# Top-32 search over halves of a score row: larger halves first, then larger and smaller together

## The chip, the core and the metric

The kernel runs on one core of a Trainium2 chip. The metric is the device time in microseconds (us) of one execution, as the median of several. PE is the matmul engine, PEld its weight loads, DVE the vector engine, ACT the scalar engine, POOL the GpSimd engine and SP the engine whose queue issues most DMAs.

## What is computed

```
# q, k, v: (B=8, H=8, S=576, D=64); TOPK = 32
scores = (1/8) * q @ k^T                         # 576 scores in a row
kth    = 32nd largest score of each row
attn   = softmax(scores where scores >= kth, else -1e9)
x      = (attn @ v) as (B*S = 4608, H*D = 512)
h      = x @ w_in                                # w_in: 512 x 2048
out    = (h * cos(h)) @ w_out                    # w_out: 2048 x 512
```

## The kernel before

**Units and slots.** The work of the attention is cut into 144 units: 128 rows of tokens by two heads. Four units, one for each pair of heads, make one block of 128 tokens, and there are 36 blocks. A loop by hand writes one slot for each unit. In slot i, `u` is unit i (its search), `w` is unit i-1 (its softmax), `x` is unit i-2 (its transposition) and `z` is a group of four units whose product with v is due, in every slot with i mod 4 = 2 from slot 10 on (slot 5 has the first group). There is no scheduler: each engine does its instructions in the order in which `slot` writes them, and waits for others by semaphores.

**A slot.** `scores` lets PE write a row's 576 scores of two heads to PSUM, the tile `sc` (columns 0 to 447) and the tile `rim` (the rest). Even slots write the scores of the next two units. `sc` has two buffers, so the second of the two waits until DVE has folded unit i. `take_scores` (L253, L257) copies the scores of unit i+1 to SBUF on ACT, the tile `s`; its copy from `rim` comes after the products with v, which also lie in `rim`. `mask` (L378) and `exponentials` (L387) are ACT's too. `split` (L410, L412) lets POOL part the finished weights into 16-bit halves; `write_halves` and `transposes` (L441, L447) send them by DMA to DRAM and back, transposed, into `ring`, on SP's queue. `values` (L475) multiplies them by v. `send` is split, write, due loads and transposition in one. Slots 0 to 5 use `turn`, a transposition on PE, in place of `send`.

**The search.** A row is folded: `fold_high` (L267, DVE) writes the larger of columns j and j+288, 288 numbers, to the second half of the tile `rest`. `fold_sum` and `fold_low` (L283, L292, POOL) make the smaller of each two from integer sums: a + b - max. In slots 8 to 10 (`BUSY`) `fold_now` (L275, DVE) makes it. Then DVE searches with MAX8 (L359, the eight largest of a row) and MATCH_REPLACE8 (L364, strikes these out; a MATCH_VALUE_LOAD goes ahead of each), each for two heads: four rounds over the 288 larger ones, which give 32, and two rounds over the 288 smaller ones, which give 16. At most 16 of the smaller can be among the 32 largest. `merge_first` and `merge_second` (L347, L352) find the 32nd largest from both sorted lists, in the next slot.

**The second part.** `ff1` (L554) and `ff2` (L630) are the products with w_in and w_out. ACT takes `ff1`'s results (L568, L570), POOL reduces them to a range (L590, L599), ACT takes the sine (L609), POOL multiplies (L616). `plan` says how many items of each kind PE gets in each slot.

**The weights.** w_in and w_out come as 64-bit numbers. In the first slots they are decoded: ACT in `decode_first` (L133, L136), DVE in `decode_second` (L151), POOL in `decode_third` (L160). In slots from 2 on, DVE's and POOL's parts are written after `topk_round(u, 2)`; in slot 0 at the slot's end and in slot 1 ahead of the last search. POOL's part of slots 0 to 9 has 3, 3, 4, 3, 4, 4, 3, 2, 2 and 2 instructions, and that of slot 11 two.

Of the kernel before, what the change touches and what calls it, by code (L numbers as in the profile page):

```python
# [10 lines left out]
F32 = mybir.dt.float32  # L11
I32 = mybir.dt.int32
# [3 lines left out]
ALU = mybir.AluOpType  # L16

P = 128
TOPK = 32
NEG = -3.4028234663852886e38  # L20
# [10 lines left out]
def kernel(  # L31
# [9 lines left out]
    nc = tc.nc  # L41
    ctx.enter_context(tc.manual_schedule())
    B, H, D, S = qT.shape
# [4 lines left out]
    NP = H // 2  # L48
    NF = DF // P
    HS = S // 2  # L50
# [33 lines left out]
    for i in range(DF // CW):  # L84
        w = consts.tile([P, NC, CW], F32, tag=f"w_in{i}", name=f"w_in{i}")
# [4 lines left out]
    w = consts.tile([P, NF, DM], F32, tag="w_out", name="w_out")  # L90
# [4 lines left out]
    BUSY = range(8, 11)  # L95
# [154 lines left out]
    def take_scores(u):  # L250
# [7 lines left out]
        if at:  # L258
            nc.scalar.copy(out=s[:, :, 0:at], in_=u["sc"][:, :, 0:at])  # L259

    def fold_high(u):

        s, sc = u["s"], u["sc"]
        if u["n"] not in BUSY:
            del u["sc"]
        u["rest"] = work.tile([P, 2, S], F32, tag="rest", name="rest", bufs=1)
        nc.vector.tensor_tensor(  # L267
            out=u["rest"][:, :, HS:S], in0=sc[:, :, 0:HS], in1=s[:, :, HS:S], op=ALU.max
        )

    def fold_now(u):

        s, sc = u["s"], u.pop("sc")
        u["low"] = work.tile([P, 2, HS], F32, tag="low", name="low", bufs=1)
        nc.vector.tensor_tensor(  # L275
            out=u["low"], in0=sc[:, :, 0:HS], in1=s[:, :, HS:S], op=ALU.min
        )

    def fold_sum(u):

        s = u["s"].bitcast(I32)
        u["low"] = work.tile([P, 2, HS], F32, tag="low", name="low", bufs=1)
        nc.gpsimd.tensor_tensor(  # L283
            out=u["low"].bitcast(I32), in0=s[:, :, 0:HS], in1=s[:, :, HS:S], op=ALU.add
        )

    def fold_low(u):

        if u["n"] in BUSY:
            return  # L290
        low = u["low"].bitcast(I32)
        nc.gpsimd.tensor_tensor(  # L292
            out=low, in0=low, in1=u["rest"][:, :, HS:S].bitcast(I32), op=ALU.subtract
        )

    dens = []
    for i in range(2):
        t = consts.tile([P, 2, 2], F32, tag=f"dens{i}", name=f"dens{i}")
# [2 lines left out]

    tops = []
    for i in range(2):
        t = consts.tile([P, 2, TOPK + 1, 2], F32, tag=f"top{i}", name=f"top{i}")
        nc.vector.memset(t[:, :, 0, 1], -NEG)
        tops.append(t)

    def topk_first(u, w):  # L310

        u["top"] = tops[u["n"] % len(tops)]
        if w:
            merge_first(w)
        if u["n"] not in BUSY:
            fold_sum(u)
        fold_high(u)
        if w:
            merge_second(w)
        if u["n"] in BUSY:  # L320
            fold_now(u)
        topk_round(u, 0, [lambda: distances(w), lambda: None] if w else ())

    def topk_round(u, rnd, between=(), ahead=None):
        top, rest, lasts = u["top"], u["rest"], TOPK // 8 - 1
        end = TOPK - 1 - 8 * rnd
        at = top[:, :, end : end - 8 if rnd < lasts else None : -1, 0]
        search(
            at, rest[:, :, HS:S] if rnd == 0 else rest[:, :, 0:HS], rest[:, :, 0:HS], rnd < lasts,
            between if rnd < lasts else (),  # L330
        )
        if rnd < lasts:
            return
        del u["rest"]
        low = u.pop("low")
        for k in range(TOPK // 16):
            more = k < TOPK // 16 - 1
            if ahead and not more:
                ahead()
            search(top[:, :, 1 + 8 * k : 9 + 8 * k, 1], low, low, more, () if more else between)  # L340

    def merge_first(u):
        n = TOPK // 2 + 1
        u["lesser"] = u["top"].rearrange("p j r i -> p j (r i)")[:, :, 2 * n : 3 * n]
        nc.vector.tensor_reduce(  # L347
            out=u["lesser"], in_=u["top"][:, :, 0:n], axis=mybir.AxisListType.X, op=ALU.min
        )

    def merge_second(u):
        nc.vector.tensor_reduce(  # L352
            out=u["top"][:, :, TOPK - 1, 1], in_=u.pop("lesser"), axis=mybir.AxisListType.X,
            op=ALU.max, negate=True,
        )

    def search(to, src, rest, more, between=()):
        for j in range(2):
            nc.vector.max(to[:, j], src[:, j])  # L359
            if between:  # L360
                between[j]()
        if more:
            for j in range(2):
                nc.vector.match_replace(rest[:, j], to[:, j], src[:, j], NEG)  # L364

    def distances(u):
        top = u.pop("top").rearrange("p j r i -> p j (r i)")
        u["less"] = top[:, :, 2 * TOPK - 1 : 2 * TOPK]
        u["nd"] = small.tile([P, 2], F32, tag="nd", name="nd")
        nc.vector.tensor_reduce(  # L370
            out=u["nd"], in_=top[:, :, 2 * TOPK - 2 : 2 * TOPK], axis=mybir.AxisListType.X, op=ALU.add
        )

    def mask(u):
# [46 lines left out]
    def turn(u):  # L421

        s = u.pop("s").rearrange("p j k -> p (j k)")
        pT = u["pT"] = ring[:, u["n"] % RING]
        for half in range(2):
            tt = ps.tile([P, 512], F32, tag="mm", name="tt", bufs=2)
            for c in range(NT):
                at = (half * NT + c) * P
                nc.tensor.transpose(tt[:, c * P : (c + 1) * P], s[:, at : at + P], ident)
            nc.scalar.copy(out=pT[:, half * NT : (half + 1) * NT], in_=tt.rearrange("p (c q) -> p c q", c=NT))  # L430
        at = 2 * NT * P
        nc.tensor.transpose(room[0][:, P : 2 * P], s[:, at : at + P], ident)
# [307 lines left out]
    def send(x):  # L740

        split(x)
        write_halves(x)
        for load, b, hp in at_send.pop(x["n"] + 2, ()):
            load(b, hp)
        transposes(x)
# [8 lines left out]
    def slot(i, u, w, x, z):  # L755
        n = (3, 4, 3, 4, 4, 3)[i] if i < NP + 2 else 2 if i != 2 * NP + 1 else 0
        if i < NP:
            for load, b, hp in at_once[i]:
                load(b, hp)
        load_weights(n, nc.sync if i < NP + 2 else nc.scalar)  # L760
        if x:
            (turn if i < NP + 2 else send)(x)
        ff["late"] = False
        topk_first(u, w)
        fold_low(u)
        topk_round(u, 1)
        topk_round(u, 2)
        if i > 1:
            decode_second(NP)
            decode_third()  # L770
        reduce_first()
        reduce_second()
        made = scored.get(i, [])
        if z:
            take_banks()
        feed(*((0, 0) if i == NP + 2 else plan[i % NP][0]))

        for m in made:
# [46 lines left out]
    def drain(w, x, z):  # L825

        take_banks()
        if x:
            send(x)
        if w:  # L830
            merge_first(w)
            merge_second(w)
            distances(w)
            mask(w)
            exponentials(w)
            sums(w)
            reciprocal(w)
        forward(2)
        if z:
            values(z)  # L840
            take_values(z)
        forward(2)
# [60 lines left out]
```

## Time and profile before

| | |
|---|---|
| median of 3 runs | 1400.27 us (1400.18 to 1404.11) |
| the profiled execution's own time | 1399.15 us |
| its span, first to last instruction | 1397.0 us |
| granted PE clock, mean over the span | 0.974 |
| PE busy | 1339.6 us, 96% |
| DVE busy | 1334.2 us, 96% |
| POOL busy | 1169.3 us, 84% |
| ACT busy | 1140.6 us, 82% |

Of the profiled execution's own time 2.15 us lie outside its span. A busy share is an average over the whole span; the stages differ, and the sums below are made by stage. Instructions of DVE overlap a little, so the mean duration of one is longer than the step from one start to the next.

### The profile page before, as it was taken

To read this page: it belongs to the slowest core of one execution; us is meant where nothing else is said; L and a number is where in the kernel's file an instruction comes from. 1 tells how busy PE (TensorE), PEld (TensorE's weight loads), DVE (VectorE), ACT (ScalarE), POOL (GpSimd) and SP (SyncE) were. 2 spreads that over 40 slices of the span, in tenths; PEclk is the share of its full clock that TensorE was granted. 3 is DMA by queue.
4 is the path that set the end of the run, shared out by engine and by line. 5 is a ranking of instruction groups with operands and counts; after the bars stand their busy time and mean duration, and the time that the engine had idled before them with its cause. 6 is when DMAs were issued, how large, how long until landed. Compare 5 with 4: busy or idle time off the path is not lost.

```text
span 1397.0 us, 43804 instructions
## 1 busy us (share of the span) xinstructions
PE 1339.6 (96%) x17024; PEld 905.7 (65%) x17024; DVE 1334.2 (96%) x5004; ACT 1140.6 (82%) x2043; POOL 1169.3 (84%) x804
## 2 busy tenths in 40 slices
PE   5558999999999999999999999999999999999998
PEld 3445666666666666666666666666666666666664
DVE  7999999999999999999999999999999999999931
ACT  7987888888888888888888888888888888888842
POOL 4778988889988888888988889888888898998820
PEclk6688999999999999999999999999999999999999
DMA  9566776777575586658756567676766566555530
GB/s 303 180 203 179 196 191 167 202 175 206 160 179 160 154 198 177 175 161 200 185 157 170 159 178 191 177 164 171 211 163 172 160 171 163 160 146 157 157 103 16
DMA packets 427487, 240.86 MB, mean 172 GB/s; under 512 B 375952, under 2 KB 392592, under 8 KB 427280
## 3 DMA queue, kind: packets, MB, share of 16 engines
q1 hardware_dynamic: 420720, 224.22, 61.0%
q10 hardware_dynamic: 6560, 13.85, 2.9%
q8 instruction: 133, 2.18, 0.7%
q14 instruction: 74, 0.61, 0.1%
HBM read 45.09 MB, written 101.19 MB: 105 GB/s over the span
## 4 chain that ended last, share of the span: by engine, by line
PE 59%; DVE 35%; ACT 2%; DMA 2%; POOL 1%; issue 1%; SPq 0%; DVEq 0%; POOLq 0%; ACTq 0%
PE o L630 23%; PE mm L554 23%; DVE top L359 16%; DVE rest L364 10%; PE rim L475 7%; PE sc L242 5%; DVE low L364 3%; DVE rest L267 3%; PE rim L242 1%; DMA ring<-rows 1%; DMA rows<-halves 1%; DVE xT L491 0%; DVE top L347 0%; DVE w_out L151 0%; DVE top L352 0%
## 5 line engine op out<-in xcount | busy, mean ns | idle before, releaser
L554 PEld LDWEIGHTS mm<-xT,w_in 128*64 128x64 f32 x9216 | 512.8, 137 | 85.1 <-issue 57.2
L554 PE MATMUL mm<-xT,w_in 128*64 128x128 f32 x9216 | 528.7, 273 | 3.2 <-DVE xT L491 2.1
L630 PE MATMUL o<-w_out,g 128*64 128x512 f32 x2304 | 520.0, 594 | 0.0
L359 DVE MAX8 top<-rest 128x8 f32<-128x288 f32 x1152 | 479.5, 452 | 0.0
L364 DVE MATCH_REPLACE8 rest<-top,rest 128x288 f32<-128x288 f32 x864 | 377.0, 444 | 0.0
L378 ACT ACTIVATE s<-s,top 128x576 f32<-128x576 f32 x288 | 207.7, 768 | 160.8 <-DVE top L352 157.8
L630 PEld LDWEIGHTS o<-w_out,g 128*64 128x64 f32 x2304 | 158.6, 137 | 254.1 <-issue 253.1
L410 POOL COPY halves<-s 128x2304 uint16<-128x2304 uint16 x140 | 294.8, 2106 | 29.1 <-ACT s L387 26.0
L359 DVE MAX8 top<-low 128x8 f32<-128x288 f32 x576 | 242.6, 452 | 0.4 <-POOL low L292 0.4
L387 ACT ACTIVATE s<-s,nd 128x576 f32<-128x576 f32 x288 | 220.5, 769 | 1.1
L292 POOL TENSOR_TENSOR low<-low,rest 128x576 int32<-128x576 int32 x141 | 199.6, 1416 | 11.1
L283 POOL TENSOR_TENSOR low<-s 128x576 int32<-128x576 int32 x141 | 199.7, 1417 | 6.1 <-ACT s L259 6.1
L599 POOL TENSOR_TENSOR x<-g,x 128x1024 f32<-128x1024 f32 x68 | 161.6, 2376 | 5.7
L242 PE MATMUL sc<-k,q 64*64 64x448 f32 (+1 forms) x1120 | 146.9, 568 | 16.9 <-DVE low L275 10.2
L616 POOL TENSOR_TENSOR g<-g,x 128x1024 f32<-128x1024 f32 x68 | 161.7, 2378 | 0.0
L475 PE MATMUL rim<-ring,v 128*64 128x128 f32 (+1 forms) x2560 | 138.3, 267 | 0.0
L475 PEld LDWEIGHTS rim<-ring,v 128*64 128x64 f32 x2560 | 129.2, 139 | 6.5 <-issue 6.0
L253 ACT COPY s<-sc 128x896 f32<-128x896 f32 (+1 forms) x144 | 128.4, 891 | 3.1 <-PE sc L242 3.1
L257 ACT COPY s<-rim 64x256 f32<-64x256 f32 (+1 forms) x280 | 102.9, 368 | 29.5 <-PE rim L475 27.9
L364 DVE MATCH_REPLACE8 low<-top,low 128x288 f32<-128x288 f32 x288 | 125.8, 446 | 0.0
L267 DVE TENSOR_TENSOR rest<-sc,s 128x576 f32<-128x576 f32 x144 | 107.7, 748 | 7.0 <-ACT s L259 6.4
L568 ACT ACTIVATE g<-mm 128x512 f32<-128x512 f32 x144 | 85.2, 592 | 25.7 <-PE mm L554 23.2
(55 smaller groups left out, 1161.8 us busy)
## 6 DMA issues: line engine op xcount, KB each, us to landing
rows<-halves SPq DMA_DIRECT2D x140, 640.0 KB, 3.5
out_dram<-ob ACTq DMA_DIRECT2D x36, 256.0 KB, 2.2
q<-in_q_dram SPq DMA_DIRECT2D x31, 288.0 KB, 4.6
st<-in_moe_w_in_dram SPq DMA_DIRECT2D x16, 512.0 KB, 5.1
v<-in_v_dram SPq DMA_DIRECT2D x32, 256.0 KB, 4.2
k<-in_k_dram SPq DMA_DIRECT2D x31, 144.0 KB, 4.2
k<-in_k_dram SPq DMA_DIRECT2D x32, 128.0 KB, 4.7
st<-in_moe_w_out_dram SPq DMA_DIRECT2D x8, 512.0 KB, 4.7
```

Source lines behind the costliest of these rows:

```text
L242: nc.tensor.matmul(to[r0 : r0 + rows, rim_bank(r0, j) if k0 else place(u["hp"], j), 0 : k1 - k0], st["q"][d, q0 : q0 + rows], st["k"][d, k ...
L283: nc.gpsimd.tensor_tensor(out=u["low"].bitcast(I32), in0=s[:, :, 0:HS], in1=s[:, :, HS:S], op=ALU.add)
L292: nc.gpsimd.tensor_tensor(out=low, in0=low, in1=u["rest"][:, :, HS:S].bitcast(I32), op=ALU.subtract)
L359: nc.vector.max(to[:, j], src[:, j])
L364: nc.vector.match_replace(rest[:, j], to[:, j], src[:, j], NEG)
L378: nc.scalar.activation(out=s[:, j], in_=s[:, j], func=AF.Prelu, bias=less[:, j], scale=1.0, alpha=FAR)
L387: nc.scalar.activation(out=s[:, j], in_=s[:, j], func=AF.Exp, bias=nd[:, j : j + 1], scale=SCALE, accum_out=den[:, j, 0:1],)
L410: nc.gpsimd.tensor_copy(out=halves[:, :, 0 : 2 * S], in_=s.rearrange("p (k h) -> p h k", h=2))
L475: nc.tensor.matmul(to[d, r], lhsT, rhs, start=(bank, j) not in begun, stop=c == NT - 1 and u in us[-2:] and r0 + rows == P,)
L554: nc.tensor.matmul(mm[r0 : r0 + D, at : at + w], w_in[f // FC][:, c, (f % FC) * P + r0 : (f % FC) * P + r0 + D], blk["xT"][:, c], start=c ...
L616: eng.tensor_tensor(out=g, in0=g, in1=x, op=ALU.mult)
L630: nc.tensor.matmul(o[r0 : r0 + D], g[:, at + r0 : at + r0 + D], w_out[f], start=f == 0, stop=f == NF - 1)
```

## The change

The four rounds become these: the first over the 288 larger numbers (now the tile `high`), whose remainder is written to the first half of `rest`; the second over that remainder, 288 wide; the third and fourth over both halves of `rest` together, 576 wide, larger and smaller. The smaller numbers are therefore read from the third round on, where they were read after the fourth. The last number found is the threshold, and `threshold` (one reduction) takes the place of the two merges.

The function `by_vector` makes DVE fold the smaller numbers also in slots 13, 17, 21 and so on (i mod 4 = 1), beside slots 8 to 10. From slot 6 on, where POOL folds, `send(x)` is now written after the folds; where DVE folds, it stays ahead of the search.

```diff
+    def by_vector(u):
+        return u["n"] in BUSY or (u["n"] > max(BUSY) and u["n"] % NP == 1)
     def fold_high(u):
...
-        u["rest"] = work.tile([P, 2, S], F32, tag="rest", name="rest", bufs=1)
+        u["high"] = work.tile([P, 2, HS], F32, tag="high", name="high", bufs=1)
         nc.vector.tensor_tensor(
-            out=u["rest"][:, :, HS:S], in0=sc[:, :, 0:HS], in1=s[:, :, HS:S], op=ALU.max
+            out=u["high"], in0=sc[:, :, 0:HS], in1=s[:, :, HS:S], op=ALU.max
         )
...
     def topk_first(u, w):
         u["top"] = tops[u["n"] % len(tops)]
+        u["rest"] = work.tile([P, 2, S], F32, tag="rest", name="rest", bufs=1)
         if w:
-            merge_first(w)
-        if u["n"] not in BUSY:
+            threshold(w)
+        if not by_vector(u):
             fold_sum(u)
         fold_high(u)
-        if w:
-            merge_second(w)
-        if u["n"] in BUSY:
+        if by_vector(u):
             fold_now(u)
-        topk_round(u, 0, [lambda: distances(w), lambda: None] if w else ())
+        search(
+            u["top"][:, :, 1:9], u["high"], u["rest"][:, :, 0:HS], True,
+            [lambda: distances(w), lambda: None] if w else (),
+        )
     def topk_round(u, rnd, between=(), ahead=None):
+        if ahead:
+            ahead()
+        some = u["rest"][:, :, 0 : HS if rnd == 1 else S]
+        search(u["top"][:, :, 1 + 8 * rnd : 9 + 8 * rnd], some, some, rnd < TOPK // 8 - 1, between)
+        if rnd == TOPK // 8 - 1:
+            del u["rest"], u["high"]
...
+    def threshold(u):
+        u["less"] = u["top"][:, :, 0:1]
         nc.vector.tensor_reduce(
-            out=u["lesser"], in_=u["top"][:, :, 0:n], axis=mybir.AxisListType.X, op=ALU.min
+            out=u["top"][:, :, 0], in_=u["top"][:, :, TOPK : TOPK + 1], axis=mybir.AxisListType.X,
+            op=ALU.max, negate=True,
         )
...
     def slot(i, u, w, x, z):
...
-        if x:
-            (turn if i < NP + 2 else send)(x)
+        if x and i < NP + 2:
+            turn(x)
+        elif x and by_vector(u):
+            send(x)
         topk_first(u, w)
         fold_low(u)
+        if x and i >= NP + 2 and not by_vector(u):
+            send(x)
         topk_round(u, 1)
         topk_round(u, 2)
         if i > 1:
             decode_second(NP)
             decode_third()
```

More of the change, by code (lines that the diff above doesn't have):

```diff
@@ L273, in fold_now @@
         s, sc = u["s"], u.pop("sc")
-        u["low"] = work.tile([P, 2, HS], F32, tag="low", name="low", bufs=1)
         nc.vector.tensor_tensor(
-            out=u["low"], in0=sc[:, :, 0:HS], in1=s[:, :, HS:S], op=ALU.min
+            out=u["rest"][:, :, HS:S], in0=sc[:, :, 0:HS], in1=s[:, :, HS:S], op=ALU.min
         )
@@ L281, in fold_sum @@
         s = u["s"].bitcast(I32)
-        u["low"] = work.tile([P, 2, HS], F32, tag="low", name="low", bufs=1)
         nc.gpsimd.tensor_tensor(
-            out=u["low"].bitcast(I32), in0=s[:, :, 0:HS], in1=s[:, :, HS:S], op=ALU.add
+            out=u["rest"].bitcast(I32)[:, :, HS:S], in0=s[:, :, 0:HS], in1=s[:, :, HS:S], op=ALU.add
         )
     def fold_low(u):
-        if u["n"] in BUSY:
+        if by_vector(u):
             return
[L291 to L294, printed above, removed]
+        low = u["rest"].bitcast(I32)[:, :, HS:S]
+        nc.gpsimd.tensor_tensor(out=low, in0=low, in1=u["high"].bitcast(I32), op=ALU.subtract)
     dens = []
@@ L303 @@
     for i in range(2):
-        t = consts.tile([P, 2, TOPK + 1, 2], F32, tag=f"top{i}", name=f"top{i}")
-        nc.vector.memset(t[:, :, 0, 1], -NEG)
-        tops.append(t)
+        tops.append(consts.tile([P, 2, TOPK + 1], F32, tag=f"top{i}", name=f"top{i}"))
     def topk_first(u, w):
         u["top"] = tops[u["n"] % len(tops)]
+        u["rest"] = work.tile([P, 2, S], F32, tag="rest", name="rest", bufs=1)
         if w:
-            merge_first(w)
-        if u["n"] not in BUSY:
+            threshold(w)
@@ L316, in topk_first @@
+        if not by_vector(u):
             fold_sum(u)
         fold_high(u)
-        if w:
-            merge_second(w)
-        if u["n"] in BUSY:
+        if by_vector(u):
             fold_now(u)
-        topk_round(u, 0, [lambda: distances(w), lambda: None] if w else ())
+        search(
+            u["top"][:, :, 1:9], u["high"], u["rest"][:, :, 0:HS], True,
+            [lambda: distances(w), lambda: None] if w else (),
+        )
     def topk_round(u, rnd, between=(), ahead=None):
-        top, rest, lasts = u["top"], u["rest"], TOPK // 8 - 1
@@ L326, in topk_round @@
[L326 to L340, printed above, removed]
@@ L344, in merge_first @@
[L344 to L347, printed above, removed]
-            out=u["lesser"], in_=u["top"][:, :, 0:n], axis=mybir.AxisListType.X, op=ALU.min
[L349 to L353, printed above, removed]
+        if ahead:
+            ahead()
+        some = u["rest"][:, :, 0 : HS if rnd == 1 else S]
@@ L366, in distances @@
     def distances(u):
-        top = u.pop("top").rearrange("p j r i -> p j (r i)")
-        u["less"] = top[:, :, 2 * TOPK - 1 : 2 * TOPK]
         u["nd"] = small.tile([P, 2], F32, tag="nd", name="nd")
         nc.vector.tensor_reduce(
-            out=u["nd"], in_=top[:, :, 2 * TOPK - 2 : 2 * TOPK], axis=mybir.AxisListType.X, op=ALU.add
+            out=u["nd"], in_=u.pop("top")[:, :, 0:2], axis=mybir.AxisListType.X, op=ALU.add
         )
@@ L830, in drain @@
         if w:
-            merge_first(w)
-            merge_second(w)
+            threshold(w)
             distances(w)
```

## The prediction

> **What bounds the kernel now.** I read the page first, then busy time by stretches of the steady part, then the chain in order of time, then the groups of DVE by shape, then the time-ordered rows of DVE and POOL at the start.
>
> ```profile
> PE 1339.6 (96%) x17024; PEld 905.7 (65%) x17024; DVE 1334.2 (96%) x5004; ACT 1140.6 (82%) x2043; POOL 1169.3 (84%) x804
> 188.59:1278.98 1090.39, 1090.13 (x14248) 737.97 (x14244) 1090.39 (x4138) 923.56 (x1649) 973.62 (x661) 1.00 0.67 174
> 188.59:224.73 36.14, 36.14 (x473) 24.54 (x469) 36.14 (x139) 30.51 (x54) 32.19 (x23) 1.00 0.67 179
> 551.88:588.61 36.73, 36.73 (x553) 25.22 (x549) 36.73 (x140) 31.10 (x58) 32.75 (x23) 1.00 0.68 171
> ```
>
> The last three rows give stretch, length, then busy PE, PEld, DVE, ACT, POOL. From 188.59 to 1278.98 us PE and DVE are both busy all the time, so the share does not say which one binds. The spacing does:
>
> ```profile
> 705.24 3.49 PE mm L554 x64
> 708.73 3.43 PE o L630 x16
> ...
> 733.86 4.08 PE rim L475 x80
> 737.94 3.43 PE o L630 x16
> 704.83 0.75 DVE L267 TENSOR_TENSOR rest<-sc,s 128x576 f32<-128x576 f32 x1
> 713.75 0.75 DVE L267 TENSOR_TENSOR rest<-sc,s 128x576 f32<-128x576 f32 x1
> 850.29 0.75 DVE L267 TENSOR_TENSOR rest<-sc,s 128x576 f32<-128x576 f32 x1
> ```
>
> PE's pieces stand end to end: 64 products of 128 columns in 3.49 us are 54.5 ns each, 16 of 512 columns in 3.43 us are 214 ns each, so 0.42 to 0.43 ns a column in both, a steady rate with no hole for a wait. A block takes PE 36.14 us where nothing makes it wait, and 36.73 where the block straddles two batches (80 more small products: 553 against 473). DVE's slots start 8.92 us apart, and four blocks (16 slots) from 704.83 to 850.29 take 145.46 us, 36.37 a block. So DVE binds by only 0.23 us a block, with PE right behind it. The 30 blocks of that stretch would take PE alone 26 x 36.14 + 4 x 36.73 = 1086.56 us; they took 1090.39. All that a faster DVE can bring there is 3.8 us.
>
> **What the change takes from DVE.**
>
> ```profile
> L491 DVE TENSOR_TENSOR xT<-rim,ring 128x256 f32<-128x256 f32 x30 | 12.0, 418 | 11.2 <-PE rim L475 10.5 <-ACT s L257 0.7
> L491 DVE TENSOR_TENSOR xT<-rim,ring 128x512 f32<-128x512 f32 x14 | 9.6, 685 | 0.0
> 57.46 0.23 DVE L347 TENSOR_REDUCE top<-top 128x34 f32<-128x68 f32 x1
> 57.60 0.75 DVE L267 TENSOR_TENSOR rest<-sc,s 128x576 f32<-128x576 f32 x1
> 58.27 0.18 DVE L352 TENSOR_REDUCE top<-top 128x2 f32<-128x34 f32 x1
> 58.38 0.46 DVE L359 MAX8 top<-rest 128x8 f32<-128x288 f32 x1
> 59.19 0.07 DVE L364 MATCH_VALUE_LOAD rest<-top,rest 128x8 f32 x1
> 60.03 0.81 DVE L359 MAX8 top<-rest 128x8 f32<-128x288 f32 x2
> 60.76 0.07 DVE L364 MATCH_VALUE_LOAD rest<-top,rest 128x8 f32 x1
> 61.61 0.81 DVE L359 MAX8 top<-rest 128x8 f32<-128x288 f32 x2
> ```
>
> From start to start, two MAX8 of 288 take 0.73 us (60.03 to 60.76) and two replacements with their loads 0.85 (60.76 to 61.61). No search of 576 stands in the trace; 256 more elements cost 267 ns in L491, 1.04 ns each, so 288 more cost 0.30, and I take 1.33 for two wide MAX8 and 1.45 for two wide replacements. Below 0.73 and 0.85 they cannot fall, as they read more; upward the bound is two narrow instructions for one, 1.46 and 1.70. The elements read stay the same, only starts are saved: before 6 x 0.73 + 4 x 0.85 = 7.78 us a slot, after 2 x 0.73 + 2 x 1.33 + 2 x 0.85 + 1.45 = 7.27, 0.51 less. The merges (0.14 and 0.11 by the same rows) become one reduction, about 0.13: 0.12 less. A slot falls from 8.92 to 8.3. DVE's fold in each fourth slot adds 0.67 (57.60 to 58.27, the step of the same shape). A block needs 36.37 - 2.5 + 0.67 = 34.5 us of DVE, under PE's 36.14 by 1.6. At the upper bounds, 0.13 and 0.25 a pair more, a slot gains 0.51 back and the block is at 36.6, just above PE.
>
> **What it costs at the start.** POOL is not free there.
>
> ```profile
> 17.07 3.79 POOL L160 TENSOR_TENSOR w_in<-w_in,st 128x512 int32<-128x512 int32 x3 [6.75 <-DVE top L347]
> 20.82 1.40 POOL L283 TENSOR_TENSOR low<-s 128x576 int32<-128x576 int32 x1
> 22.30 1.41 POOL L292 TENSOR_TENSOR low<-low,rest 128x576 int32<-128x576 int32 x1
> 23.74 0.82 DVE L359 MAX8 top<-low 128x8 f32<-128x288 f32 x2 [0.36 <-POOL low L292]
> 32.89 1.38 DVE L151 TENSOR_SCALAR w_in<-w_in 128x1024 int32<-128x1024 int32 x2
> 34.41 5.04 POOL L160 TENSOR_TENSOR w_in<-w_in,st 128x512 int32<-128x512 int32 x4 [1.29 <-ACT s L257]
> 43.12 1.02 DVE L151 TENSOR_SCALAR w_in<-w_in 128x1024 int32<-128x1024 int32 x2
> 88.81 0.75 DVE L267 TENSOR_TENSOR rest<-sc,s 128x576 f32<-128x576 f32 x1
> 109.12 0.75 DVE L267 TENSOR_TENSOR rest<-sc,s 128x576 f32<-128x576 f32 x1
> ```
>
> In slots 0 to 7 POOL ends a slot with 3 or 4 decodings (3.75 us for three, 17.07 to 20.82; 5.0 for four), which wait for DVE's L151, and the next slot's folds queue behind them (2.89 from 20.82 to their end). Already now slot 1 waits 0.36 us for them at its fifth pair of searches. With the change DVE needs them two rounds earlier, while L151 comes 1.1 later in its slot (behind a wide round). A loop closes: third round and its replacement (1.33 + 1.45), L151 (0.9 to 1.3 by number and size), decodings (3.75 or 5.0), folds (2.89), and 0.15 for two hand-overs: 10.5 us with three, 12.1 with four, against slots of 10.15 (88.81 to 109.12 is two). Followed from slot 0 (L151 done 0.5 earlier, at 16.4; folds done at 23.25), the third round of slots 1 to 7 starts at 23.3, 33.8, 45.8, 56.3, 68.4, 80.4 and 90.9, and slot 8 folds at 90.9 + 2.78 + 0.7 + 1.64 = 96.0, where it was 88.81: 7.2 later. In slots 8 and 9 DVE folds by itself, so they gain 0.55 each, and slot 10 starts 6.1 later. PE is not the bound there, so nothing hides this, and its dense part starts with slot 10's fold. If POOL's decodings were out of the way, the same slots would give 6.0 us instead (ten times 0.6).
>
> **The steady part after.** With 34.5 on DVE, PE is late next, at 36.14. POOL loses 2.8 us a block (1.40 + 1.41), ACT nothing. POOL's folds must be done by the third round, 3.9 us into a slot (57.60 to 61.61, less the step of L352, which goes) where they had two rounds more; alone they take 2.9 from the slot's start, so they fit if POOL is free then. `send` stands behind them on POOL and SP, its loads too, but not in slots 13, 17, ..., which send the last unit of a block. I take 2.4 of the 3.8 us, as some of PE's waits are for `ring`, which a later `send` of the unit before does not shorten:
>
> ```profile
> PEld rim L475 <- DMA ring<-rows: 2.3, 4, 1.0
> ```
>
> **Slots 11 to 14.**
>
> ```profile
> 120.69 0.75 DVE L267 TENSOR_TENSOR rest<-sc,s 128x576 f32<-128x576 f32 x1
> 127.08 2.54 POOL L160 TENSOR_TENSOR w_out<-w_out,st 128x512 int32<-128x512 int32 x2 [1.97 <-issue]
> 129.58 2.37 POOL L616 TENSOR_TENSOR g<-g,x 128x1024 f32<-128x1024 f32 x1
> 137.18 1.03 POOL L590 TENSOR_SCALAR x<-x 128x1024 f32<-128x1024 int32 x1
> 140.61 2.10 POOL L410 COPY halves<-s 128x2304 uint16<-128x2304 uint16 x1
> 142.66 0.40 POOL L412 COPY halves<-rden 128x256 uint16<-128x256 uint16 x1
> 143.08 2.97 DMA rows<-halves
> 146.18 6.40 DMA ring<-rows
> 152.63 4.08 PE rim L475 x68
> ```
>
> Here POOL is the chain: unit 11 is split by 143.06, and PE waits for its `ring` until 152.58. After, slot 11 starts near 127.3 (120.69 + 6.1, and 0.5 for the longer last round, which follows `take_values`); folds to 130.1, split of unit 9 to 132.6, the two decodings wait for L151 and end at 137.3, the product L616 at 139.7, folds of slot 12 at 142.6 (DVE waits 1.9 us), split of unit 10 at 145.1, L590 and L599 (3.43, from 137.18 to 140.61) at 148.6, split of unit 11 at 151.1; its rows queue on SP behind unit 10's transposition (151.8) and `ring` lands near 161.5: 8.9 late, 2.8 more than PE. Bounds: 0 if POOL catches up, 4 if the DMAs crowd as at 146.18.
>
> The sum: 6.1 + 2.8 - 2.4 = 6.5 us on the profiled execution's own 1399.15, or 1405.65. That execution lies 1.1 under the median, so I give 1400.27 + 6.5 = 1406.8. With the bounds of the three terms (4.6 to 7.6, 0 to 4, -3.9 to 0.5) this case reaches from 1401 to 1412.4.
>
> **A rule against this reading of PE.** PE's busy share in the steady row is 1090.13 of 1090.39 and its pieces stand end to end. The Trainium skill, Perfetto Trace Analysis, section Identifying the Most-Contended Engine, says to go for the engine of highest occupancy, and that a matmul busy share is no good measure of nearness to the roofline, while for Vector it is fair. By that rule DVE, busy in all of 1090.39, is the engine to relieve. The steady rate of 0.42 to 0.43 ns a column in both shapes says that PE has no slack here, whatever its share is worth.
>
> **Rivals.**
>
> *Even.* POOL catches up in slots 11 to 14 and the steady part gives all 3.8: 6.1 - 3.8 = 2.3, 1402.6. For it: POOL has 2.8 us less in each later block. Against: the queue of slots 11 to 13 holds no less work.
>
> *Faster, no loop at the start.* The folds reach DVE in time; then -6.0 - 2.4 = -8.4, 1391.9. This decides if DVE's third round waits under 0.6 us in slots 1 to 7. Against it stands the 0.36 us that slot 1 waits even now, two rounds later.
>
> *Faster, PE has slack.* The block follows DVE's 34.5: 33 blocks by 1.6 to 1.9 us are about 60, 1347 with the start's loss. Against it: the rate of a column. (The Trainium skill's rule above would have it so.)
>
> *Slower by far, `ring` late in every block.* If splits queue behind folds so that values wait 0.5 us in each of 31 blocks, 15.5 more: 1422. It decides once unit 4k+3's `ring` lands over 36 us after the values before; the four waits of 2.3 us say that it is near at times, the lighter POOL speaks against it.
>
> *Slower, wide searches dear.* If each of the 24 wide instructions of a block costs 0.1 more than its elements, DVE binds at 36.9: 0.8 by 33 blocks, 26 more, 1433. L491's even step per element speaks against it. That the change would not do what it says is only this.
>
> **How the numbers follow.** Chances: the forecast 0.53, even 0.22, no loop 0.13, PE slack 0.02, `ring` late 0.07, dear searches 0.03. The range takes in forecast, even and no loop: 1391.5 to 1413, the likeliest one's own being 1401 to 1412.4. About 0.3%, 4.2 us, is what a measurement of this kernel can tell from no change. Faster by more: 0.15; within: 0.22; slower by more: 0.63.
>
> **What would show it.** Right: DVE waits for POOL's L292 ahead of the third round by 1 to 3 us in each of slots 1 to 7, the fold of slot 10 near 115, later blocks at 36.14 on PE with DVE idle some 1.6 us in each. Wrong: slot 10 before 109, DVE still without holes after 200 us, or blocks above 36.4.

## The result, and the profile after

The changed kernel takes 1494.52 us (median of 4 runs, 1485.12 to 1500.53), the kernel before 1400.22 beside it (4 runs). The ratio is 1.066, 95% interval 1.0594 to 1.0728 (the ratios here are those of the record and need not equal the quotient of two medians): 94 us slower, where 6.5 were forecast. The profiled execution of the changed kernel took 1498.98 us with a span of 1497.2.

The profile page of the changed kernel: busy time of the engines, then the chain of work that ended last, by engine and by line.

```profile
PE 1376.7 (92%) x17024; PEld 937.2 (63%) x17024; DVE 1269.6 (85%) x3739; ACT 1135.7 (76%) x2043; POOL 1071.4 (72%) x738
PE 64%; DMA 16%; DVE 8%; POOL 3%; ACT 2%; issue 1%; SPq 0%; POOLq 0%
PE o L608 26%; PE mm L532 23%; DMA ring<-rows 14%; PE rim L453 11%; DVE top L339 4%; PE sc L242 3%; DVE rest L344 3%; DMA rows<-halves 2%; POOL halves L388 1%; PE rim L242 1%; DVE high L271 1%; POOL rest L285 0%; POOL rest L294 0%; POOL x L577 0%; ACT s L257 0%
```

DVE did become lighter, by 65 us. But neither DVE nor PE is now busy all the time, and the third largest line of the chain is a DMA, `ring<-rows`, with 14%, where it had 1% before. The same 30 blocks as in the prediction, and a block in which PE waits for nothing (it lies across two batches) beside one in which it does (stretch, length, then busy PE, PEld, DVE, ACT, POOL, the granted clock, the DMA share and GB/s):

```profile
201.69:1372.15 1170.46, 1121.11 (x14251) 764.48 (x14245) 1040.32 (x3092) 919.23 (x1651) 884.99 (x601) 0.98 0.65 162
240.09:276.81 36.72, 36.72 (x553) 25.08 (x548) 34.74 (x105) 30.59 (x56) 29.66 (x21) 1.00 0.74 168
276.81:319.29 42.48, 39.28 (x472) 27.20 (x468) 34.60 (x104) 30.57 (x56) 29.52 (x21) 0.92 0.67 167
```

The 30 blocks grew from 1090.39 to 1170.46 us, so 80.1 of the span's 100.2 are lost here, 2.7 a block. DVE does 34.6 to 34.7 us of work in a block, as forecast (34.5), and is idle for the rest. The values of slot 18 start at 201.69 instead of 188.59, which is 13.1 more; the other 7 come after the 30 blocks, where the same waits go on. The waits of the changed kernel (us in total, times, longest):

```profile
PEld rim L453 <- DMA ring<-rows: 64.7, 31, 4.3
DVE xT L469 <- ACT s L257: 117.7, 27, 8.8
POOL rest L285 <- DVE rden L378: 239.3, 84, 9.3
DVE top L339 <- POOL rest L294: 14.9, 8, 2.7
```

PE's values products wait for `ring` 31 times, up to 4.3 us (before: 4 times, 2.3 us in all). DVE in turn waits for the values, at `xT` (by way of ACT's copy from `rim`, L257, which comes after them). POOL waits for DVE to end a slot before it may fold again, with whatever stands behind the fold in its queue. These are three sides of one loop, which the chain in order of time shows (start, length, what):

```profile
1022.08 7.03 DMA ring<-rows
1029.16 5.77 PE rim L453 x68
...
1035.33 0.38 ACT s L257
1035.73 0.69 DVE xT L469
1036.42 0.67 DVE top L339
...
1038.00 0.67 DVE high L271
...
1046.46 1.43 POOL rest L285
1047.96 1.43 POOL rest L294
1049.39 2.05 POOL halves L388
...
1051.77 1.02 POOL x L568
1052.87 1.97 POOL x L577
...
1055.18 2.10 POOL halves L388
...
1057.65 4.85 DMA rows<-halves
1062.57 6.12 DMA ring<-rows
1068.73 4.08 PE rim L453 x68
```

Read it from the top. `ring` lands and PE makes the values. `take_values` (L469) on DVE needs them and stands ahead of the last wide round, so slot 4k+3 can start only at 1038.00. It takes 8.4 us. Then slot 4k+4 starts and POOL may fold (L285 writes into `rest`, whose one buffer DVE has just left). The split of unit 4k+2 (L388 at 1049.39) now stands behind these folds; two products of the reduction (L568, L577) follow, and only then the split of unit 4k+3 (L388 at 1055.18). Its rows and its transposition end when PE has stood still for 1.3 us. One turn is 39.6 us here (1029.16 to 1068.73), and PE's 36.14 lie beside it with time to spare.

I measured the parts of that turn in three kernels, the last of them that of the first experiment below, with all sends ahead of the search again: the mean over the same 30 blocks of the differences between the starts or ends named. "Lands to values" is negative where PE began with the part that needs no late `ring` and then waited.

| mean, us | before | changed | send first |
|---|---|---|---|
| values start to start of slot 4k+3 | 7.55 | 10.11 | 7.42 |
| slot 4k+3 on DVE | 8.93 | 8.37 | 8.36 |
| start of slot 4k+4 to end of split 4k+3 | 9.66 | 11.42 | 9.62 |
| end of that split to its `ring` landing | 9.03 | 11.12 | 8.68 |
| `ring` lands to values start | 1.18 | -2.00 | 2.14 |
| block | 36.35 | 39.02 | 36.22 |

The split of unit 4k+2 ends 0.35 us after the start of slot 4k+4 before, 5.36 after it in the changed kernel. POOL before, around such a slot, which starts at 1041.06 (start, length; in brackets the idle time before and what ended it): the copy of unit 4k+2, its short second copy, the first fold, and the copy of unit 4k+3.

```profile
1037.63 2.11 POOL L410 COPY halves<-s 128x2304 uint16<-128x2304 uint16 x1
1041.01 0.40 POOL L412 COPY halves<-rden 128x256 uint16<-128x256 uint16 x1 [1.26 <-DVE rden L400]
1041.37 1.41 POOL L283 TENSOR_TENSOR low<-s 128x576 int32<-128x576 int32 x1
...
1048.26 2.11 POOL L410 COPY halves<-s 128x2304 uint16<-128x2304 uint16 x1
```

### The profile page after: what moved, and what is told of

Its sections match the earlier page's. It is cut to its first block, busy times and chain, and to the rows that moved or that the text cites. A ratio compares the mean times of both kernels' runs of the same rounds, so it can differ in the third digit from the quotient of the medians.

```text
span 1497.2 us, 42516 instructions
## 1 busy us (share of the span) xinstructions
PE 1376.7 (92%) x17024; PEld 937.2 (63%) x17024; DVE 1269.6 (85%) x3739; ACT 1135.7 (76%) x2043; POOL 1071.4 (72%) x738
## 4 chain that ended last, share of the span: by engine, by line
PE 64%; DMA 16%; DVE 8%; POOL 3%; ACT 2%; issue 1%; SPq 0%; POOLq 0%
PE o L608 26%; PE mm L532 23%; DMA ring<-rows 14%; PE rim L453 11%; DVE top L339 4%; PE sc L242 3%; DVE rest L344 3%; DMA rows<-halves 2%; POOL halves L388 1%; PE rim L242 1%; DVE high L271 1%; POOL rest L285 0%; POOL rest L294 0%; POOL x L577 0%; ACT s L257 0%
## 5 line engine op out<-in xcount | busy, mean ns | idle before, releaser
L339 DVE MAX8 top<-rest 128x8 f32<-128x576 f32 (+1 forms) x864 | 533.7, 651 | 14.9 <-POOL rest L294 14.9
L285 POOL TENSOR_TENSOR rest<-s 128x576 int32<-128x576 int32 x108 | 153.1, 1418 | 300.9 <-DVE rden L378 239.3
L344 DVE MATCH_REPLACE8 rest<-top,rest 128x288 f32<-128x288 f32 (+1 forms) x576 | 337.9, 596 | 0.0
L388 POOL COPY halves<-s 128x2304 uint16<-128x2304 uint16 x140 | 294.5, 2104 | 12.5 <-DMA rows<-halves 12.5
L257 ACT COPY s<-rim 64x256 f32<-64x256 f32 (+1 forms) x280 | 102.8, 367 | 153.2 <-PE rim L453 151.6
L242 PE MATMUL sc<-k,q 64*64 64x448 f32 (+1 forms) x1120 | 151.3, 565 | 15.8 <-DVE rest L278 8.4
L577 POOL TENSOR_TENSOR x<-g,x 128x1024 f32<-128x1024 f32 x68 | 160.8, 2364 | 5.7
L294 POOL TENSOR_TENSOR rest<-rest,high 128x576 int32<-128x576 int32 x108 | 152.7, 1414 | 8.5
L453 PE MATMUL rim<-ring,v 128*64 128x128 f32 (+1 forms) x2560 | 158.4, 290 | 0.0
L453 PEld LDWEIGHTS rim<-ring,v 128*64 128x64 f32 x2560 | 149.0, 155 | 7.2 <-issue 6.6
L469 DVE TENSOR_TENSOR xT<-rim,ring 128x256 f32<-128x256 f32 (+1 forms) x44 | 21.7, 506 | 135.9 <-ACT s L257 117.7
L339 DVE MAX8 top<-high 128x8 f32<-128x288 f32 x288 | 127.1, 456 | 3.7
L344 DVE MATCH_REPLACE8 rest<-top,high 128x288 f32<-128x288 f32 x288 | 125.5, 444 | 0.0
```

Source lines behind the costliest of these rows:

```text
L242: nc.tensor.matmul(to[r0 : r0 + rows, rim_bank(r0, j) if k0 else place(u["hp"], j), 0 : k1 - k0], st["q"][d, q0 : q0 + rows], st["k"][d, k ...
L285: nc.gpsimd.tensor_tensor(out=u["rest"].bitcast(I32)[:, :, HS:S], in0=s[:, :, 0:HS], in1=s[:, :, HS:S], op=ALU.add)
L388: nc.gpsimd.tensor_copy(out=halves[:, :, 0 : 2 * S], in_=s.rearrange("p (k h) -> p h k", h=2))
L453: nc.tensor.matmul(to[d, r], lhsT, rhs, start=(bank, j) not in begun, stop=c == NT - 1 and u in us[-2:] and r0 + rows == P,)
L577: nc.gpsimd.tensor_tensor(out=x, in0=g, in1=x, op=ALU.subtract)
```

## Experiments

Where nothing else is said, a kernel is the changed one with the edit shown; times are medians, with the ratio to the kernel before and its 95% interval. Slots are counted modulo 4; a slot i sends unit i-2, so slots 4k+4 send unit 4k+2, and slots 4k+5 (13, 17, ..., which always send first) unit 4k+3.

**All sends ahead of the search again.**

```diff
-        if x and i < NP + 2:
-            turn(x)
-        elif x and by_vector(u):
-            send(x)
+        if x:
+            (turn if i < NP + 2 else send)(x)
...
-        if x and i >= NP + 2 and not by_vector(u):
-            send(x)
```

> The changed kernel, with send(x) at the head of every slot again, as before the change; search and by_vector stay as changed. Theory A, the ring loop: values of a block end, ACT copies rim, DVE multiplies xT and does the last round (3.1 us), slot 4k+3 follows (8.3), then POOL does folds, split of unit 4k+2, reduction and split of unit 4k+3 (11.2 together from the start of slot 4k+4), then rows and ring by DMA (10.7) and the values of the next block (4.1 to 5.8): about 39 us, over PE's 36.14. With send first, the 2.1 us copy of unit 4k+2 is done ahead of the slot's start, and the loop loses 2.1 to 2.5 us: a block takes 36.3 to 36.9 us, and the time is 1405 to 1425, of which 7 to 11 is lost in the first ten slots (slots 6 and 7 now split ahead of their folds, 2.5 each). Rival B, the wide searches or DVE's fold in slots 13, 17, ... cost more than their elements: a block stays at 38 to 39 us and the time near 1490. Rival C, the rows of unit 4k+3 crowd with the ring of unit 4k+2, whatever the order on POOL: a block stays above 38.

Measured: 1410.05 us (1409.07 to 1411.55), ratio 1.0073 (1.0056 to 1.009). The 30 blocks in its windows:

```profile
202.87:1289.37 1086.50, 1086.50 (x14250) 738.21 (x14245) 1040.21 (x3091) 920.98 (x1651) 888.61 (x601) 1.00 0.67 174
```

They take 1086.50 us, PE busy in all of it; PE alone had been put at 1086.56 in the prediction. POOL around the start of slot 4k+4, which is at 1015.31 in this kernel (start, length; in brackets the idle time before and what ended it):

```profile
1012.52 2.11 POOL L388 COPY halves<-s 128x2304 uint16<-128x2304 uint16 x1
1015.33 0.40 POOL L390 COPY halves<-rden 128x256 uint16<-128x256 uint16 x1 [0.69 <-DVE rden L378]
1015.69 1.42 POOL L285 TENSOR_TENSOR rest<-s 128x576 int32<-128x576 int32 x1
1017.19 1.41 POOL L294 TENSOR_TENSOR rest<-rest,high 128x576 int32<-128x576 int32 x1
1019.09 1.05 POOL L568 TENSOR_SCALAR x<-x 128x1024 f32<-128x1024 int32 x1 [0.50 <-ACT x L548]
1020.23 2.38 POOL L577 TENSOR_TENSOR x<-g,x 128x1024 f32<-128x1024 f32 x1
1022.55 2.11 POOL L388 COPY halves<-s 128x2304 uint16<-128x2304 uint16 x1
```

The copy of unit 4k+2 runs in the time in which POOL would only wait for DVE to end its slot. Folds and products are the same; the split of 4k+3 ends 9.6 us after the slot's start and not 11.4. Of the theories, A, the loop through `ring`, gave this time; a block is 0.08 us under its range. What remains of the loss lies at the start (values of slot 18 at 202.87).

**Send first in one slot of four more (4k+4).**

```diff
-        elif x and by_vector(u):
+        elif x and (by_vector(u) or i % NP == 0):
...
-        if x and i >= NP + 2 and not by_vector(u):
+        if x and i >= NP + 2 and not (by_vector(u) or i % NP == 0):
```

> The changed kernel, with send(x) ahead of the search also in slots 12, 16, 20, ... (i mod 4 = 0), and in no other slot. These are the slots in which unit 4k+2 is sent, one slot ahead of the last unit of a block. Theory A: the loop passes POOL only in this slot, so this one move of four gives what send first in all slots gives in the steady part, 36.3 to 36.9 us a block; the first slots keep the loss of about 7 us: 1403 to 1420. Rival B (dear searches or folds): 38 to 39 us a block, near 1490. Rival D, it is the general lateness of all sends, each with its loads, on SP and POOL: only a third of the gain, 37.5 to 38.3 us a block, 1450 to 1475.

Measured: 1443.02 us (1438.06 to 1446.74), ratio 1.0305 (1.0282 to 1.0329), 37.23 a block. None of the three ranges held it. Its waits:

```profile
POOL halves L388 <- DMA rows<-halves: 48.9, 35, 4.8
DVE top L339 <- POOL rest L294: 75.2, 40, 4.1
```

The loop became shorter, but unit 4k+1 was still sent late, and its rows had not left the one `halves` buffer when the split of 4k+2 wanted it. That split then stood on POOL ahead of the folds and held them, and DVE's third round waited for the folds: slot 4k+4 took 10.3 us instead of 8.4. Moving this one send back only moved the wait.

**The old search with the sends behind.** The kernel before, with nothing but the order of the sends changed:

```diff
-        if x:
-            (turn if i < NP + 2 else send)(x)
+        early = i in BUSY or (i > max(BUSY) and i % NP == 1)
+        if x and i < NP + 2:
+            turn(x)
+        elif x and early:
+            send(x)
...
+        if x and i >= NP + 2 and not early:
+            send(x)
```

> The kernel before, with its old search and merges, and only send(x) moved behind the folds as in the change (slots 8 to 10 and 13, 17, ... keep it first; POOL folds in these 13, 17, ... too). Theory A: the loop is 4.1 (values) + 2.1 (rim copy, xT, last narrow pair, sums) + 8.9 (slot 4k+3) + 11.2 (POOL) + 10.7 (rows, ring) = 37.0 us, more where PE's clock falls after a long wait: 37 to 38.5 us a block against 36.35, so 1420 to 1465. Rival B (the new search is what costs): 1395 to 1405.

Measured: 1485.74 us (1475.83 to 1494.19), ratio 1.061 (1.0561 to 1.0659), 38.48 a block, and the same wait:

```profile
PEld rim L475 <- DMA ring<-rows: 57.5, 32, 4.5
```

So the moved `send` makes nearly the whole loss without any new search. A's range held the block (37 to 38.5), at its upper end, but not the time, which is 20.7 us over it.

**`take_values` behind the last round, from slot 11.**

```diff
-        if ahead:
+        if ahead and u["n"] <= max(BUSY):
             ahead()
...
+        if ahead and u["n"] > max(BUSY):
+            ahead()
```

> The changed kernel, with take_values(z) (the xT products, which wait for the block's values) written after the last round of the search from slot 11 on, in place of ahead of it. Nothing changes on POOL, in the sends or the DMAs. Theory A: the last round (1.5 us with sums) is then done while values still run, and falls out of the loop: a block loses about 1.5 us, 39.0 to 37.5, some 45 us in all: 1440 to 1460. Rival C (crowding of rows with the ring before) and rival B (dear searches): no change, 1485 to 1500.

Measured: 1430.43 us (1425.87 to 1434.9), ratio 1.0217 (1.0192 to 1.0243), 36.75 a block.

```profile
PEld rim L455 <- DMA ring<-rows: 19.7, 17, 2.7
```

With the sends left behind the searches, taking DVE's last round and threshold out of the loop (the values' start to slot 4k+3 falls from 10.11 to 6.43 us) gives 64 us of the 94 back. The loop passes through `xT`, as A says; the time is 10 us under A's range. PE also kept its full rate in the values of every block here, which took 18.7 us more in the changed kernel (see the end).

**One send behind, that of slots 4k+6.** The expectation names the unit wrongly: this edit leaves the send behind in the slots that split unit 4k, not 4k+2.

```diff
-        elif x and by_vector(u):
+        elif x and (by_vector(u) or i % NP in (0, 3)):
...
-        if x and i >= NP + 2 and not by_vector(u):
+        if x and i >= NP + 2 and not (by_vector(u) or i % NP in (0, 3)):
```

> The changed kernel with the send behind the search in one slot of four only (the slot that splits unit 4k+2); the three others send first. If the loss comes from the last two splits of a block standing one behind the other late (the split of 4k+2 behind the folds of its slot, 4k+3 right after), 4k+3's ring stays late by part: 36.4 to 37.5 a block, 1412 to 1445. If what made the kernel with the send first in two slots of four slow (1443) was only the late send of 4k+1, whose rows kept the halves buffer, this one falls to 36.2 to 36.5 a block, 1405 to 1415.

Measured: 1411.15 us (1409.9 to 1413.64), ratio 1.0081 (1.0066 to 1.0096), 36.28 a block: a late send of unit 4k alone costs 2 us in 30 blocks. Beside the kernel that sends first also in slots 4k+4 it also says that the late send of 4k+1 was what held the `halves` buffer there.

**One send behind, that of slots 4k+4 (unit 4k+2).**

```diff
-        elif x and by_vector(u):
+        elif x and (by_vector(u) or i % NP in (2, 3)):
...
-        if x and i >= NP + 2 and not by_vector(u):
+        if x and i >= NP + 2 and not (by_vector(u) or i % NP in (2, 3)):
```

> The changed kernel with one send left behind the search: that of slots 4k+4, which split unit 4k+2; the three others send first. If the last two splits of a block, one behind the other, carry the loss (slot 4k+4's folds, its split, two of PE's products' steps on POOL, then the split of 4k+3, 11 us after the slot starts), the ring of 4k+3 lands some 2 us after PE is ready for it in most blocks, as in the changed kernel: 38 to 39 us a block, 1455 to 1490 in all. If it is the sum of the later splits of all three units that matters, one alone costs a third: 36.5 to 37.2 a block, 1410 to 1440. If only the order at the head of 4k+4 matters little, 36.2 to 36.4 and 1410, like the kernel that leaves unit 4k's send behind.

Measured: 1488.49 us (1482.21 to 1497.44), ratio 1.0635 (1.0598 to 1.0671), 38.35 a block. This one send, once a block, is the main cause: with it alone the loss is 88 us, while late sends of 4k and 4k+1 without it cost 43 (the second experiment) and of 4k alone 11, most of that at the start. The 30 blocks take 60 us more than before, of the changed kernel's 80. The parts of the turn are those of the changed kernel (split of 4k+3 ends 11.36 us after the slot's start, `ring` 10.79 later), and so is the wait below. One wait is not: the split of unit 4k, sent first here, waits 41.5 us in 15 of the 30 blocks until the rows of the unit before have left `halves`, and DVE 6.7 for the folds behind it.

```profile
PEld rim L453 <- DMA ring<-rows: 54.4, 30, 3.8
```

**DVE's own folds in slots 1 to 10.** The start by itself:

```diff
-    BUSY = range(8, 11)
+    BUSY = range(1, 11)
```

> The changed kernel with DVE making its own smaller half in slots 1 to 10 instead of 8 to 10, and nothing else. If the start's loss is DVE's third round waiting for POOL's folds, slot 10 folds at 107.5 to 109 instead of 115.75 and its waits for the folds in slots 1 to 7 are gone; the blocks stay at 38.5 to 39.1 and the whole at 1480 to 1492. If the decodings themselves hold the start, slot 10 folds at 112 or later.

Measured: 1484.04 us, one run; 38.61 a block, both in the range. DVE waits for L294 once in the whole trace (1.8 us). Slot 9 folds at 98.68, and at 106.24 in the changed kernel.

So 7.6 us are back by slot 9: the loss of slots 1 to 8 was DVE's wait for POOL's folds. But slot 10 folds at 113.43, only 2.3 earlier than in the changed kernel, and the range of 107.5 to 109 was missed. The time lies where the rival, the decodings themselves, had put it (112 or later). What the trace shows is a late load: one load of weights, issued at 89.1, took 13.6 us to land; ACT stood still 6.0 us for it, with the exponentials behind it in its queue, and DVE's last round of slot 9 waited 3.0 us for these. With the sends first as well (the next kernel), that load took 7.7 us, ACT waited 0.2 us for it and slot 10 folds at 106.44, so the decodings need not hold the start. More on that load below.

**Both together: all sends first and ten slots folded on DVE; the same without DVE's folds after slot 10; and with DVE's folds in slots 1 to 14.** The edits are the first one and `BUSY`; the second kernel has `return u["n"] in BUSY` in `by_vector`, the third `range(1, 15)`.

> The changed kernel with the sends of every slot back ahead of the searches, and DVE making its own smaller half in slots 1 to 10 instead of 8 to 10, so that no search at the start waits for POOL. If the two losses are the two named (ring late in the blocks; DVE waiting for POOL's folds behind the decodings at the start), both are gone: the fold of slot 10 near 108 us (before 109.12, changed 115.75), the blocks at 36.2, and the whole 1393 to 1402, at or under the kernel before. If the start's loss is rather POOL's decodings themselves, which wait for DVE's shifts a wide round later, slot 10 stays over 112 and the whole at 1406 to 1411, as with the sends first alone.

Measured: 1400.59 us (1395.26 to 1406.26, 12 runs), ratio 1.0002 (0.9987 to 1.0017), 36.22 a block.

> As the kernel with sends first and DVE's own folds in slots 1 to 10, but after slot 10 POOL makes every fold, also in slots 13, 17 and so on. DVE's work a block falls by 0.67 us, POOL's rises by 2.8. If PE alone sets the block (36.14) the steady part is the same as there, within 2 us, as long as POOL keeps up; if POOL's line (folds, splits, decodings' rest) then becomes late for the third round or for a split, blocks grow by 0.3 to 1.4 us, 10 to 40 us in all.

Measured: 1400.21 us (1396.92 to 1402.41, 11 runs), ratio 1.0003 (0.9994 to 1.0012), 36.22 a block: once the sends are first, 2.8 us more on POOL cost nothing, and 0.67 less on DVE bring nothing.

> The kernel with all sends first and DVE's own folds in slots 1 to 10, with DVE folding in slots 11 to 14 as well. There slot 12 still waits 3.9 us for POOL's folds, on the path to the values of slot 14 (153.46 us, before 151.21). Taking the wait away and adding two folds of 0.67 on that path should bring those values to about 151 and the whole 2 to 3 us under the kernel with ten such slots: 1396.5 to 1399, blocks at 36.22. If POOL's splits and not the folds set slots 11 to 14, the values stay at 153 and the time within 1 us of 1400.6.

Measured: 1398.14 us (1393.34 to 1407.48, 11 runs) beside 1400.48 of the kernel before (15 runs), ratio 0.9998 (0.9982 to 1.0013), 36.22 a block. In its profiled execution the values of slot 14 start at 148.84 (153.46 with ten such slots, 151.21 before). The loss is undone in all three, but none is faster than the kernel before by more than can be measured.

**The last of them once more**, since its runs lie 14 us apart:

> The kernel with all sends first and DVE's own folds in slots 1 to 14 once more, unchanged, to see where its executions differ (1393.3 to 1407.5 us; the one profiled so far was the shortest, with a span of 1391.6, the values of slot 18 at 188.2, 30 blocks of 36.217 and 116.9 from there to the end). If the start makes the difference, the values of slot 18 come later than 188.2 by what the span is longer; if rings land late in some blocks, the mean of the blocks is above 36.22; otherwise it is the end.

Measured: 1409.0 us, one run, with a span of 1407.1; 36.216 a block, the values of slot 18 at 199.81 (188.20 in the execution of 1393.34). So 11.6 of the 15.5 us lie at the start, and 4 at the end. The chain has them in one load:

```profile
86.48 17.43 DMA st<-in_moe_w_out_dram
```

A load of these weights is issued between 86.5 and 89.7 us in each of the 13 profiled executions. From issue to landing it took 4.1 to 5.7 us in seven of them (before 5.7, changed 4.7, the execution of 1393.34 5.7) and 7.7 to 17.4 in six, among these the kernel with ten folds on DVE (7.7), the one without folds after slot 10 (11.0) and the start alone (13.6). Two of the six have the slow start (the one that sends first also in slots 4k+4, with 11.4, and the one with `take_values` behind, with 9.3), so it does not hang on a faster start alone. What holds the load up was not found, and is open; between the two executions of this kernel it makes most of the difference, and it is about as large as what the start could give.

## Why the prediction was wrong, by its steps

**The start: right.** The third rounds of slots 1 to 7 were forecast to start at 23.3, 33.8, 45.8, 56.3, 68.4, 80.4 and 90.9. Measured, with the wait for POOL in brackets:

```profile
23.48 1.42 DVE L339 MAX8 top<-rest 128x8 f32<-128x576 f32 x2 [2.73 <-POOL rest L294]
34.09 1.42 DVE L339 MAX8 top<-rest 128x8 f32<-128x576 f32 x2 [1.23 <-POOL rest L294]
46.20 1.42 DVE L339 MAX8 top<-rest 128x8 f32<-128x576 f32 x2 [2.45 <-POOL rest L294]
...
91.74 1.42 DVE L339 MAX8 top<-rest 128x8 f32<-128x576 f32 x2 [1.23 <-POOL rest L294]
```

Slot 10 folds at 115.75, 6.6 us late where 6.1 were forecast. The loop through the decodings was worked out there step by step, and came out to 0.2 us in slot 1 and 0.8 in slot 7, a tenth of a microsecond more in each slot.

**DVE's costs: right.** The wide searches of the changed kernel, grouped by shape (busy, mean ns):

```profile
L339 DVE MAX8 top<-rest 128x8 f32<-128x576 f32 x576 | 416.7, 753 | 14.9 <-POOL rest L294 14.9
L344 DVE MATCH_REPLACE8 rest<-top,rest 128x576 f32<-128x576 f32 x288 | 212.3, 747 | 0.0
L339 DVE MAX8 top<-rest 128x8 f32<-128x288 f32 x288 | 117.1, 449 | 0.0
```

288 elements more cost 304 ns (753 less 449), where 0.30 us were taken from `xT`'s shapes. A slot is 8.37 us where 8.3 were forecast; dear searches are out.

**PE next at 36.14: right, but not reached.** With the sends first, each of the 30 blocks takes 36.14, or 36.71 across batches, and together they take 3.9 us less than before, the whole of the 3.8 put down as DVE's share. The Trainium skill, Perfetto Trace Analysis, section Identifying the Most-Contended Engine, says to optimize the engine of highest occupancy first, which by its rule is DVE here. In these runs 65 us less work on DVE brought 3.9 in the 30 blocks, since PE was as full.

**Slots 11 to 14: mis-sized.** `ring` for slot 14 was forecast to land at 161.5 and landed at 164.9. From slot 11's folds on, POOL followed the forecast with one shift: folds at 130.70, slot 12's folds done at 146.0, unit 11 split at 154.5, each 3.4 later than written down. The shift comes from slot 10, whose values the forecast leaves out of these slots. They waited for `ring` and then ran slowly, and slot 11 had to wait for them through `take_values` (start, length, what):

```profile
114.71 6.47 DMA ring<-rows
121.23 6.31 PE rim L453 x68
```

The values of slot 18 then start 13.1 us late, where 8.9 (6.1 + 2.8) were forecast.

**The steady part: wrong, and this is the failing step.** It said that the sends go behind the folds "but not in slots 13, 17, ..., which send the last unit of a block", and gave -2.4 us on the ground that a wait for `ring` is one that a later send of the unit before neither shortens nor, as I took it, lengthens. It does lengthen it: in place of the 2.4 us gained, the 30 blocks lost 80.1, at 39.02 a block, over the 36.4 that the prediction named as a sign of being wrong. The runs show four steps. (1) The split of unit 4k+2 no longer fills POOL's idle time before the fold but stands between the folds and the products, so the split of 4k+3, in the same queue, ends 1.8 us later (11.42 against 9.66). (2) The two units' DMAs now follow each other closely (the splits end 6.1 us apart, 9.3 before), and 4k+3's `ring` needs 11.1 us from its split instead of 9.0. Every kernel that leaves unit 4k+2 behind has 10.3 to 11.1 there, the others 8.7 to 9.4. SP's queue (start, length) has the transposition of 4k+2 just ahead of the rows of 4k+3:

```profile
1054.86 2.66 SPq L425 DMA_TRANSPOSE ring<-rows  x1
1057.65 0.48 SPq L419 DMA_DIRECT2D rows<-halves  x1
1062.57 3.08 SPq L425 DMA_TRANSPOSE ring<-rows  x1
```

By the same 30 blocks, of the 2.1 us 0.4 go until SP issues the rows (0.44 against 0.03), 0.6 into the write of the rows (4.14 against 3.50, with the transposition of 4k+2 still under way in all 30 blocks, in 9 before) and 1.1 into the transposition (6.46 against 5.40). That last part starts 1.3 us or more after the transposition of 4k+2 has landed, so what slows it stays open; the loads that `send` carries on SP's queue moved with it, and no run moved them alone. (3) Late values hold slot 4k+3 through `take_values`, which the change puts ahead of a round twice as wide; so a late `ring` makes the next one late, and the loss is not made up in the next block; taking `take_values` behind that round gave 64 us back. (4) After some of the pauses PE's values products run at a lower clock, inside the loop (18.7 us in all).

**The rival.** *Slower by far, `ring` late in every block* is what came. Its point of decision was right: 4k+3's `ring` lands 41.0 us after the values before (the first four means of the table), 35.2 before and 34.1 with the sends first; the limit was put at 36. It had a chance of 0.07 and a price of 0.5 us a block, where 2.7 came. Neither was worked out: the prediction has only the four waits of 2.3 us for it. The lighter POOL, which was held against it, does not help a queue whose order makes it wait: POOL stood idle 239.3 us for DVE. Worked out as the start's loop was, it would have stood out: 1.2 us of slack in the turn before, against 1.8 us later on POOL, is 0.6 us a block short, about the rival's price. The rest of the 2.7 came with steps 2 to 4.

## To carry to other kernels

Where a step is moved behind another in an in-order queue, follow everything that stands behind it to the next turn of the loop, not only the step itself, and add up the whole turn against the engine that is meant to hide it. Here a copy that sat in POOL's waiting time cost nothing there, and 1.8 us of the turn two places further on. And an engine that is lighter than before can still be the late one: what counts is when it may start.

## What had not been expected of the hardware

PE's clock fell after some quite short pauses. The changed kernel's values products, 64 of 128 columns, after a wait of 2.01 us and after one of 1.32 us, and the granted clock (0.67, the third number from the end) over the first; over the second it is 1.00:

```profile
1029.16 0.43 PE L453 MATMUL rim<-ring,v_tail 64*64 64x128 f32 x4 [2.01 <-DMA ring<-rows]
1029.53 5.38 PE L453 MATMUL rim<-ring,v 128*64 128x128 f32 x64
1068.73 0.44 PE L453 MATMUL rim<-ring,v_tail 64*64 64x128 f32 x4 [1.32 <-DMA ring<-rows]
1069.09 3.71 PE L453 MATMUL rim<-ring,v 128*64 128x128 f32 x64
1029.50:1034.70 5.20, 5.20 (x66) 5.18 (x66) 0.81 (x3) 0.00 (x0) 2.62 (x2) 0.67 0.59 183
```

Over the 30 blocks, all of the 19 in which PE went up to 2.2 us from one product's start to the next one's kept the full rate (3.54 us for these 64 products from the first start to the last, 4.3 for the 144 narrower ones of a block across two batches), and all of the 11 from 2.28 us on took 4.86 to 6.6. Together these 11 took 18.7 us more than at the full rate. The Trainium skill, TensorE: Matmul & The Clock Gate, section The HAM clock gate, gives half rate after an idle window of about 3.4 us, free-running; here 2.0 us without a product were enough, and the measurement decides. In the other kernels the border is not sharp: with 4k+2's send alone behind, a pause of 2.0 us was followed by the lower rate and one of 3.32 us was not, and with `take_values` behind none was, up to 2.76 us. So the length of the pause alone does not decide it.
